# Attention and a Silu feed-forward on one core: all sums on VectorE, a redrawn order, and seven products for the first matmul of the last three batches

## The chip, the cores and the metric

One core of a Trainium2 chip. The time is that of one execution on the device, in microseconds (us), as the median of several runs. The profile is a hardware trace of one execution, whose span runs from the first to the last instruction of the program.

## The reference

Attention over 8 batches and 12 heads, 448 tokens of 64 values each, and then a feed-forward layer over the 3584 tokens with 768 values each:

```python
scores = q @ k.T / sqrt(64)              # per batch and head, 448 x 448
attn   = exp(scores - max) / sum(exp)
x      = attn @ v                        # heads side by side: 3584 x 768
h      = x @ w_in                        # 768 -> 2048
out    = (h * sigmoid(h)) @ w_out        # 2048 -> 768
```

Inputs and outputs are float32; the kernel loads them as float16 and sums in float32 in PSUM.

## The kernel before

**The work.** A unit is one batch with four of the twelve heads. Its k and q are loaded (L316, L322) and turned in 32x32 blocks on VectorE (L363, L374). Scores (L384) are matmuls with 32 rows of the array, four side by side; ScalarE takes Exp of two heads at once into a tile E (L409, 128x896). `attend` (L433) multiplies E by ones (part 0, the row sums) and by V (parts 1 and 2). To save part 0 one matmul in four, the first two chunks of E are added beforehand (`plan_esum`, two sums of 128x896 for a unit). VectorE inverts the sums (L455 to L460) and scales the result into xT (L466). Before this change the E sums could go to VectorE or GpSimd, whichever the plan found free.

**First feed-forward matmul.** `Plain` computes 128 rows of h for one batch as six matmuls of 128x128 by 448 (L486), then Tanh on ScalarE (L499) and a gate on VectorE, (tanh + 1) * x into G or, for some last 128 tokens of a pair of batches, X (L502). There are 16 such pieces in a batch. `Fold` is another way, which the code holds but does not use while `PLAIN = 8`: a 2x2 block form with seven products instead of eight, each of three matmuls of 224 columns, and eight folds in a batch. It needs four sums on the batch's x (`plan_t`), four on every slice of w_in (`plan_w_in_sums`, the tiles SI), and for each fold a copy, four additions with an operand in PSUM (y, c22, c12, c21) on VectorE, and a subtraction z on GpSimd (`ZENG`). The sums of w_in were made before this change too, although nothing read them.

**Second feed-forward matmul.** `Quad` does two tiles of 128 tokens by the same seven-product form: 56 matmuls of 384 columns (L805), four sums on G (tiles S, in two halves of 128x512, `plan_sums`), sums of w_out once (tiles TO, 16 sums of 128x768), and additions t and p on VectorE. In `VPS = (3, 4)` the third and fourth sums on G may go to GpSimd. Results go out through tiles t (L511, L515, L517) and stores (L546). All sums are issued by the helper `tt`, so they share line L511 and are told apart by their tiles.

**The order.** Every engine runs its instructions in the order in which the program emits them. That order comes from a plan at the end of the kernel: a class `Order` keeps a clock of its own, estimated durations (`mm`, `act`, `vec`, `half`, `pool`) and a time at which each engine is free, and starts the ready operation with the earliest time plus bias. It also keeps which buffers and PSUM banks are free. An operation of kind ANY goes to ScalarE or VectorE, one of kind VP to VectorE or GpSimd. Loads are issued on GpSimd, behind its sums. At the end all operations are emitted in the order of their planned start. The estimates set the order alone; on the chip, semaphores decide when each operation runs.

**Silu and the tables.** With `b >= SILU` a fold ends with ScalarE's Silu instead of Tanh and a gate. Silu isn't in the table of Exp and Tanh, so the plan issues no scores while more than `QB = 4` of a batch's Silu operations are left (`silu_phase`).

Of the kernel before, what the change touches and what calls it, by code (L numbers as in the profile page):

```python
# [18 lines left out]
DMA_RATE = 0.37  # L19
DMA_TAIL = 1.0  # L20
# [3 lines left out]


# [54 lines left out]
class Op:  # L80


    def __init__(self, eng, busy, emit, deps=(), bias=0.0, tail=HOP, then=None, table=None):
        self.eng, self.busy, self.emit = eng, busy, emit
        self.deps, self.bias, self.tail, self.then = list(deps), bias, tail, then
        self.table = table
        self.done = None
# [5 lines left out]
class Order:  # L93


    def __init__(self):
        self.now = 0.0
        self.free = {"PE": 1.2, "ACT": 2.1, "DVE": 1.2, "POOL": 1.2}
        self.wait = {"ACT": [], "DVE": [], "ANY": [], "POOL": [], "VP": []}
        self.pool = []  # L100
        self.dma_free = 0.0
        self.out = []
        self.mode = None
        self.table, self.loose = 0, True
        self.busy = {e: 0.0 for e in self.free}

    def add(self, op):
        self.wait[op.eng].append(op)
        return op

# [3 lines left out]
    def start(self, op, eng=None):  # L114
        eng = eng or op.eng
        busy = op.busy[eng] if isinstance(op.busy, dict) else op.busy
        if isinstance(op.busy, dict):
            self.emit(lambda: op.emit(eng))
        else:
            self.emit(op.emit)  # L120
        if op.table is not None:
            if op.table != self.table:
                self.table = op.table
                busy += TABLE
        self.free[eng] = self.now + busy
        self.busy[eng] += busy
        op.done = self.now + busy + op.tail
        if op.then:
            op.then(op.done)
# [7 lines left out]
    def load(self, mb, emit, ring=None):  # L137
        op = Op("POOL", 0.58, emit)
        self.pool.append((op, mb, ring))
        return op  # L140

    def step(self):

        soon = []
        for eng in ("ACT", "DVE"):
            if self.free[eng] > self.now:
                soon.append(self.free[eng])
                continue
            best, other = None, None
            for kind in (eng, "ANY") if eng == "ACT" else (eng, "ANY", "VP"):  # L150
                for op in self.wait[kind]:
                    at = op.ready()
                    if at is None:
                        continue
                    if at > self.now:
                        soon.append(at)
                    elif eng == "ACT" and op.table not in (None, self.table):
                        if (other is None or at < other[0]) and (self.table == 0 or self.loose):
                            other = (at, op)
                    elif best is None or at + op.bias < best[0]:  # L160
                        best = (at + op.bias, op)
            if other:
                best = other if not best or self.table == 0 and other[0] < self.now - PATIENCE else best
                if best is not other:
                    soon.append(other[0] + PATIENCE + 0.01)
            if best:
                self.wait[best[1].eng].remove(best[1])
                self.start(best[1], eng)
                soon.append(self.free[eng])
        work = None  # L170
        for kind in ("POOL", "VP"):
# [12 lines left out]
        elif self.pool:  # L184
            op, mb, ring = self.pool[0]
            at = 0.0
            if ring is not None:
                at = ring()
            if at is not None and at <= self.now:
                self.pool.pop(0)  # L190
                self.start(op)
                self.dma_free = max(self.dma_free, self.now + 1.5) + mb / DMA_RATE
                op.done = self.dma_free + DMA_TAIL
# [7 lines left out]
def kernel(  # L201
# [10 lines left out]

# [20 lines left out]
    DEFER, DITEM = .3, .1  # L233
    SUMS, EKEEP, ESENG = (0, 1), 2, 'VP'
# [4 lines left out]
    PLAIN = 8  # L239
    SILU = 8  # L240
# [3 lines left out]
    W_OUT_AT = NG * len(PIECES) + 6  # L244
    W_OUT_GAP = 2
# [21 lines left out]
    SI = {m: const.tile([128, HC, DFF // 2], FP16, name=f"SI{m}") for m in (1, 2, 4)}  # L267
# [5 lines left out]
    T_s = const.tile([128, 3, HC, S // 2], FP16, name="T")  # L273
    f_s = [const.tile([128, 3, S // 2], FP32, name=f"f_{i}") for i in range(NF)]
# [7 lines left out]
    def bank(i):  # L282
        return P_s[i // 2][:, 0] if i < 4 else B_s[i - 4]
# [16 lines left out]
    def rows_of(n, c):  # L300
        return KROWS[c] if form(*units[n][:2]) == "lone" else 128

# [114 lines left out]
    def attend(n, part, a, es, sums):  # L417
# [6 lines left out]
        for c in chunks:  # L424
            rest = c == NCH - 1 and what != "lone"
# [159 lines left out]
    def plan_k(b, hg):  # L585
        ld_k[(b, hg)] = od.load(1.2 * MB * TPP, lambda: load_k(b, hg), ringed("rk"))

    def plan_q(n):
        ld_q[n] = od.load(1.2 * MB * (units[n][3] - units[n][2]), lambda: load_q(n), ringed("rq"))
# [101 lines left out]
    VPS = (3, 4)  # L691
    WENG = 'VP'
# [14 lines left out]
    def bulk(out, u, w, how, deps, bias):  # L707
# [7 lines left out]
        return od.add(Op(WENG, busy, lambda eng: tt(out, u, w, how, eng), deps, bias))  # L715
# [34 lines left out]
    plan_w_in_sums()  # L750
# [3 lines left out]
    class Quad:  # L754
# [59 lines left out]
        def run(self):  # L814
# [5 lines left out]
            if m == 5:  # L820
# [3 lines left out]
                "PE", (i1 - i0) * mm(n), lambda: self.emit(m, a, m in (1, 5, 6), i0, i1), tail=PE_OUT  # L824
# [13 lines left out]
            def add(name, out, x, y, deps, then=None):  # L838
                ev[name] = od.add(
                    Op("DVE", vec(n), lambda: tt(out, x, y, ALU.add), deps, SLOW, then=then)  # L840
                )

            if m == 1:
                ev["p1"] = od.add(
                    Op("ANY", {"ACT": act(n), "DVE": vec(n)}, lambda e: copy(e, p, W), [op], SLOW)
# [5 lines left out]
            elif m == 6:  # L851
                add("y", W, Q, r, [op, ev["c11"]])
            elif m == 7:
# [9 lines left out]
    class Fold:  # L863
# [66 lines left out]
        def run(self):  # L930
# [14 lines left out]
            op = Op("PE", HC * mm(n), lambda: self.emit(m, a, c0, m in (1, 7)), tail=PE_OUT)  # L945
# [3 lines left out]
            def add(name, eng, out, u, w, how, deps, then=None):  # L949
                busy = vec(n) if eng == "DVE" else 0.12 + 0.00215 * n  # L950
                ev[name] = od.add(
                    Op(eng, busy, lambda: tt(out, u, w, how, eng), deps, SLOW, then=then)
# [3 lines left out]
            if m == 5:  # L956
# [4 lines left out]
                        lambda e: copy(e, F[:, 0:2], src), [op], SLOW,  # L961
                    )
                )
            elif m == 6:
                add("y", "DVE", y, A[:, n : 2 * n], p1, ALU.add, [op])
# [3 lines left out]
            elif m == 3:  # L969
                c12 = add("c12", "DVE", A[:, n : 2 * n], A[:, n : 2 * n], p1, ALU.add, [op])  # L970
                self.finish(A[:, 0 : 2 * n], self.f, [c12], True)
            elif m == 4:
                Bq = bank(self.banks[1])[:, 0:n]
                k = self.banks[1]
                c21 = add("c21", "DVE", p5, Bq, p5, ALU.add, [op, ev["z"]], lambda at: banks.give(k, at))
                self.finish(F[:, 1:3].rearrange("p i n -> p (i n)"), self.f + HF, [c21], False)
            if m in (6, 7) and self.at >= 5 and "c22" not in ev:
                Bq = bank(self.banks[1])[:, 0:n]
                add("c22", "DVE", y, Bq, y, ALU.add, [self.last7, ev["y"]] + [ev["z"]])

        def finish(self, src, ff, deps, psum):
# [9 lines left out]
            if b < SILU:  # L991
# [4 lines left out]
                        -0.3, tail=0.2, table=0,  # L996
# [3 lines left out]
                for lo, hi, dst, at in g_parts(b, 0, S):  # L1000
# [7 lines left out]
                            [last, clear], -4,  # L1008
# [5 lines left out]
            for lo, hi, dst, at in g_parts(b, 0, S):  # L1014
# [6 lines left out]
                        deps + [clear], -2, tail=0.2, table=1,  # L1021
# [14 lines left out]
    def plan_t(b):  # L1036
# [12 lines left out]
        def sums(out, u, w, deps):  # L1049
            return od.add(  # L1050
                Op("DVE", half(HC * n), lambda: tt(out, u, w, ALU.subtract), deps, SLOW + 2)
# [40 lines left out]
    def plan_sums(qd):  # L1092
# [7 lines left out]
        while sums_at[qd] < 4:  # L1100
# [16 lines left out]
            for f0 in (0, 4):  # L1117
# [9 lines left out]
                else:  # L1127
# [7 lines left out]
                        deps, SUM,  # L1135
# [7 lines left out]
    def tile_quad(qd):  # L1143
# [34 lines left out]
        def write(r, c, src, place, deps, then):  # L1178
            if r == 0:
# [5 lines left out]
                        deps, -4,  # L1185
# [21 lines left out]
    class Plain:  # L1207
# [20 lines left out]
        def run(self):  # L1228
# [4 lines left out]
            op = Op("PE", 2 * mm(t1 - t0), lambda: ffn1_plain(b, f, t0, t1, a, c0, c0 + 2), tail=PE_OUT)  # L1233
# [7 lines left out]
            done = od.add(Op("ACT", act(t1 - t0), lambda: tanh(x, th), [op], -0.3, tail=0.2, table=0))  # L1241
# [5 lines left out]
            for lo, hi, dst, at in g_parts(b, t0, t1):  # L1247
# [5 lines left out]
                    [done], -4,  # L1253
# [38 lines left out]
    def qk_at():  # L1292
# [6 lines left out]
        s = [max(banks.free[2 * y], banks.free[2 * y + 1]) for y in ys]  # L1299
# [5 lines left out]
    def run_qk():  # L1305
# [17 lines left out]
        )  # L1323
        done = []
# [8 lines left out]
        for y in ys:  # L1333

            def then(at, y=y):
# [11 lines left out]
                    table=0,  # L1347
                )
# [3 lines left out]
        if c in SUMS and c == SUMS[-1] and per_burst(n) == 1 and ys[-1] == 1:  # L1352
            plan_esum(n)
# [3 lines left out]
    def plan_esum(n):  # L1357
# [3 lines left out]
        at = sum_at[n] = e_slots.take(od.now)  # L1361
        made = sum_op[n] = []
        kr = rows_of(n, SUMS[-1])
        nq = 32 * (units[n][3] - units[n][2])
        for y in range(2):
            hs = slice(2 * y, 2 * y + 2)
            for i, c in enumerate(SUMS[1:]):
                u = e_at[n][SUMS[0]] if i == 0 else at
# [5 lines left out]
                            lambda eng, u=u, w=e_at[n][c], hs=hs: tt(  # L1374
                                E_s[at][0:kr, hs, 0:nq], E_s[u][0:kr, hs, 0:nq],
                                E_s[w][0:kr, hs, 0:nq], ALU.add, eng,
                            ),
                            deps, -2,
# [6 lines left out]
    def lent():  # L1385
        if not qk_seq or silu_phase() or LEND and e_slots.when(1) is None:
            return 0, 2
# [9 lines left out]

    def m_when(n):
        more = lent()
        at = sorted(banks.free[i] for i in (*M, *more))[n - 1]  # L1400
        return None if at == NEVER else at

    def m_take():
        more = lent()
        i = min((*M, *more), key=lambda i: (banks.free[i] > od.now, i < 4, banks.free[i]))
        assert banks.free[i] <= od.now
# [3 lines left out]
    def av_data():  # L1410
# [7 lines left out]
        if part == 0 and n in sum_op:  # L1418
            first = len(SUMS) - 1
# [18 lines left out]
    def run_av():  # L1438
# [5 lines left out]
        sums = SUMS if n in sum_op else ()  # L1444
        count = NCH - (len(sums) - 1 if sums and part == 0 else 0)
        op = Op("PE", count * mm(nq) + 0.013, lambda: attend(n, part, a, es, sums), tail=PE_OUT)
# [18 lines left out]
    def after_av(n, part, op, nq, a):  # L1465
        b, hg, g0, g1 = units[n]
        if part == 0:
# [3 lines left out]
            for step, busy in enumerate((nq / 960.0 + 0.13, 0.2, nq / 960.0 + 0.13)):  # L1471
# [5 lines left out]
                    -10,  # L1477
                )
# [4 lines left out]
        else:  # L1483
# [5 lines left out]
            def then(at):  # L1489
# [10 lines left out]
                then=then,  # L1500
            )
# [35 lines left out]
    def moe_pick(hold):  # L1537
# [3 lines left out]
        for item in moe[:60]:  # L1541
# [10 lines left out]
            at = max([at] + room)  # L1552
            need = 0
# [12 lines left out]
        return None, soon  # L1566

# [70 lines left out]
    for _, _, fn in sorted(od.out, key=lambda x: x[:2]):  # L1638
        fn()
# [30 lines left out]
```

The softmax here doesn't subtract the row's maximum and nothing guards it: scores larger than these inputs give would overflow.

## Time and profile before

| | |
|---|---|
| median of 3 runs | 447.63 us (444.66 to 449.26) |
| span of the profiled execution | 440.4 us |
| mean granted TensorE clock | 0.979 |
| sums on GpSimd, 128x896 / 128x512 / 128x384 (mean ns) | 1922 / 1157 to 1265 / 902 to 988 |
| the same shapes on VectorE, least ns | 604 / 355 / 344 |
| matmuls 128x448 of the plain pieces | 672, in 132.9 us |

"Busy" is time in which an engine executes. A busy TensorE is not one at its peak, since its matmuls are pipelined and their ends are modelled; spacing from start to start is the better measure of one. In the lists of groups, the time after the second bar is idle time of the engine ahead of those instructions, and the name after the arrow is whoever ended it. The engines are named PE (TensorE), DVE (VectorE), ACT (ScalarE), POOL (GpSimd) and SP (SyncE).

### The profile page before, as it was taken

The page shows a single profiled execution, that of the slowest core. Times are in us where ns is not written, and L with a number is a line of the kernel's source. Part 1 is how long each engine was busy: PE and PEld are TensorE (multiplying, and loading weights), DVE is VectorE, ACT ScalarE, POOL GpSimd, SP SyncE. Part 2 cuts the span into 40 slices and gives each one's busy share as a digit, 9 for nine tenths or more (in the row PEclk, how much of TensorE's full clock was granted, in tenths as well). Part 3 has the DMA queues.
Part 4 walks back from the last instruction along what each step waited for, and adds up shares of the span by engine and source line. Part 5 has one row for each costly group of instructions (what it writes and reads, how often), then busy time and mean ns, then how long its engine had stood idle before and what let it go on. Part 6 is the DMA issues. An engine that isn't in the chain of part 4 may idle for free.

```text
span 440.4 us, 9748 instructions
## 1 busy us (share of the span) xinstructions
PE 410.0 (93%) x3853; PEld 208.8 (47%) x3853; DVE 288.6 (66%) x565; ACT 233.8 (53%) x356; POOL 209.3 (48%) x277
## 2 busy tenths in 40 slices
PE   8998878999939999999999999999999999899985
PEld 7665544334315434544554434544453555455453
DVE  3536798777899776577557974587559635834751
ACT  3885757788800768466544755456856124214310
POOL 6575898977686354087204951065306100502510
PEclk9998989899988999999999999999999999999999
DMA  7999408599914456056510853118300130022023
GB/s 111 118 152 204 67 6 106 75 183 151 201 28 69 115 89 117 1 75 106 106 49 12 122 93 84 28 18 128 75 1 2 49 92 5 19 66 61 0 50 95
DMA packets 38750, 34.46 MB, mean 78 GB/s; under 512 B 11952, under 2 KB 37936, under 8 KB 38704
## 3 DMA queue, kind: packets, MB, share of 16 engines
q0 software_dynamic: 27952, 22.82, 37.0%
q1 hardware_dynamic: 9984, 10.24, 8.6%
q10 hardware_dynamic: 768, 0.79, 0.7%
q8 instruction: 30, 0.49, 0.4%
q14 instruction: 16, 0.13, 0.1%
HBM read 45.61 MB, written 11.01 MB: 129 GB/s over the span
## 4 chain that ended last, share of the span: by engine, by line
PE 60%; DVE 5%; DMA 2%; SPq 1%; issue 1%; POOL 1%; ACT 0%; DVEq 0%
PE p L486 24%; PE p L805 24%; PE p L433 7%; PE s L384 4%; DVE S L511 2%; DMA rk<-in_k_dram 1%; DVE E L511 1%; SPq L546 1%; DMA out_dram<-t 1%; DVE t L511 0%; POOL V L330 0%; DVE p L511 0%; DVE QT L374 0%; DVE G L502 0%; ACT th L499 0%
## 5 line engine op out<-in xcount | busy, mean ns | idle before, releaser
L409 ACT ACTIVATE E<-s 128x896 f16<-128x896 f32 (+1 forms) x172 | 148.6, 916 | 68.3 <-PE s L384 67.3
L486 PE MATMUL p<-xT,w_in_t 128*128 128x448 f16 (+1 forms) x864 | 156.9, 335 | 4.2 <-DVE G L502 3.2
L486 PEld LDWEIGHTS <-w_in_t 128*128 128x128 f16 x864 | 82.1, 99 | 76.9 <-issue 19.1
L502 DVE SCALAR_TENSOR_TENSOR G<-th,p 128x448 f16<-128x448 f16 (+2 forms) x144 | 75.7, 534 | 54.6 <-ACT th L499 54.1
L499 ACT ACTIVATE th<-p 128x448 f16<-128x448 f32 (+1 forms) x144 | 70.4, 507 | 63.7 <-PE p L486 60.5
L805 PE MATMUL p<-w_out_t,G 128*128 128x384 f16 x304 | 58.0, 327 | 1.9 <-DVE p L511 1.9
L384 PE MATMUL s<-QT,KT 32*128 32x448 f16 (+4 forms) x864 | 56.7, 343 | 3.0 <-ACT E L409 2.6
L511 POOL TENSOR_TENSOR G<-G 128x512 f16<-128x512 f16 x21 | 25.6, 1227 | 64.9 <-DVE S L511 64.3
L805 PEld LDWEIGHTS <-G 128*128 128x128 f16 x416 | 38.6, 98 | 36.1 <-issue 12.0
L330 POOL DMA_DIRECT2D V<-in_v_dram x88 | 48.9, 562 | 13.7 <-PE p L433 8.4
L515 ACT COPY t<-p 128x384 f32<-128x384 f32 x39 | 18.6, 479 | 69.3 <-PE p L805 67.0
L805 PE MATMUL p<-TO,S 128*128 128x384 f16 x192 | 39.3, 340 | 11.1 <-DVE S L511 7.6
L433 PE MATMUL p<-E,V 128*32 128x448 f16 (+2 forms) x848 | 43.9, 344 | 1.4 <-DVE xT L466 1.4
L805 PEld LDWEIGHTS <-S 128*128 128x128 f16 x280 | 25.8, 100 | 37.7 <-issue 15.5
L511 POOL TENSOR_TENSOR E<-E,E 128x896 f16<-128x896 f16 x18 | 34.6, 1922 | 18.0 <-ACT E L409 17.6
L511 DVE TENSOR_TENSOR t<-p,t 128x384 f32<-128x384 f32 x42 | 23.0, 549 | 29.3 <-PE p L805 26.6
L466 DVE SCALAR_TENSOR_TENSOR xT<-p,t 128x448 f16<-128x448 f32 (+1 forms) x53 | 29.8, 565 | 13.4 <-PE p L433 12.3
L384 PEld LDWEIGHTS <-KT 32*128 32x128 f16 (+2 forms) x864 | 17.6, 98 | 30.7 <-issue 29.0
L433 PEld LDWEIGHTS <-V 128*32 128x32 f16 (+1 forms) x864 | 20.3, 98 | 22.5 <-issue 12.4
L363 DVE STREAM_TRANSPOSE KT<-rk 128x256 f32<-128x256 f32 (+3 forms) x48 | 16.7, 385 | 19.6 <-DMA rk<-in_k_dram 19.6
L511 POOL TENSOR_TENSOR G<-X,G 128x512 f16<-128x512 f16 x4 | 4.9, 1216 | 46.2 <-DVE S L511 46.2
L455 DVE STREAM_TRANSPOSE t<-p 128x448 f32<-128x448 f32 (+1 forms) x27 | 15.9, 589 | 14.2 <-PE p L433 14.0
(62 smaller groups left out, 358.2 us busy)
## 6 DMA issues: line engine op xcount, KB each, us to landing
out_dram<-t SPq DMA_DIRECT2D x208, 48.0 KB, 1.6
rk<-in_k_dram POOLq DMA_DIRECT2D x24, 224.0 KB, 4.7
rq<-in_q_dram POOLq DMA_DIRECT2D x21, 224.0 KB, 5.4
w_out_t<-in_moe_w_out_dram POOLq DMA_DIRECT2D x8, 384.0 KB, 8.9
V<-in_v_dram POOLq DMA_DIRECT2D x43, 64.0 KB, 3.3
V<-in_v_dram POOLq DMA_DIRECT2D x40, 48.0 KB, 2.7
w_in_t<-in_moe_w_in_dram POOLq DMA_DIRECT2D x16, 96.0 KB, 4.7
w_in_t<-in_moe_w_in_dram POOLq DMA_DIRECT2D x8, 192.0 KB, 8.0
```

The source lines that it names most:

```text
L330: nc.gpsimd.dma_start(out=V[32 * x : 32 * (x + 1), hs, 0:count, :], in_=v[b, hs].rearrange("h (i g) d -> i h g d", g=TPP)[:, :, first : fi ...
L363: nc.vector.transpose(out=kt.rearrange("p c x i -> p x c i")[:, x:y, 0:count], in_=t[:, first : first + count * (y - x)].rearrange("p (x c ...
L384: nc.tensor.matmul(out=P_s[s_pair][p0 : p0 + 32 * (x1 - x0), h % 2, at : at + nq], lhsT=KT[(b, hg)][32 * h : 32 * (h + 1), c, x0:x1, :, e] ...
L409: nc.scalar.activation(out=E_s[e_i][0:kr, 2 * y : 2 * y + 2, 0:nk], in_=P_s[s_pair][0:kr, :, 0:nk], func=AF.Exp, scale=attn_scale,)
L433: nc.tensor.matmul(out=bank(a)[32 * h : 32 * (h + 1), 0:nq], lhsT=w, rhs=E_s[sum_at[n] if part == 0 and c in sums else es[c // per_burst(n)]][
L466: nc.vector.scalar_tensor_tensor(out=x_s[xi][:, cc % HC, 32 * g0 : 32 * g1], in0=bank(a)[:, 0:nq], scalar=0.5, in1=t_s[ti][:, 0:nq], op0=A ...
L486: nc.tensor.matmul(out=bank(a)[:, 0 : t1 - t0], lhsT=w_in_t[:, cc, 128 * f : 128 * (f + 1)], rhs=x_s[x_at[(b, cc // HC)]][:, cc % HC, t0:t ...
L499: nc.scalar.activation(out=th, in_=src, func=AF.Tanh)
L502: (nc.vector if eng == "DVE" else nc.gpsimd).scalar_tensor_tensor(out=out, in0=th, scalar=1.0, in1=x, op0=ALU.add, op1=ALU.mult)
L511: e.tensor_tensor(out=out, in0=a, in1=b, op=op)
L515: nc.scalar.copy(out=out, in_=in_)
L805: nc.tensor.matmul(out=bank(a)[:, 0 : self.n], lhsT=lhs(i), rhs=rhs(i), start=(start and i == 0), stop=(i == last), skip_group_check=True,)
```

## The change

It has four parts.

1. **All fp16 sums go to VectorE**: E sums, sums on G, of w_in and of w_out. GpSimd keeps loads, memsets and the small fp32 subtraction z of a fold. The aim is that the two engines don't hold each other up.
2. **The first feed-forward matmul of batches 5, 6 and 7 goes by seven products** (`PLAIN = 5`), to shorten TensorE's work, and ends in Silu (`SILU = 5`), so that VectorE has no gates there.
3. **The plan knows more**: at most 8 loads are open at a time and each lands at other estimated times; while VectorE and GpSimd would use their shared access the plan starts neither on top of the other; a PSUM tile in use by one engine isn't given to another. The order of all instructions follows from it.
4. **Small settings**: w_out is loaded one unit earlier and its halves in succession, `DEFER` is 0.15 instead of 0.3, and the second half of each score tile in PSUM can be lent to feed-forward work.

```diff
-DMA_RATE = 0.37
-DMA_TAIL = 1.0
+DMA_RATE = 0.4
+DMA_LAG = 2.4
+DMA_OPEN = 8
...
+    def locked(self, tiles, eng):
+
+        return max((t for i in tiles for e, t in self.lock[i].items() if e != eng), default=0.0)
...
+                    elif self.locked(op.tiles, eng) > self.now:
+                        soon.append(self.locked(op.tiles, eng))
+                    elif eng == "DVE" and op.port and self.port["POOL"] > self.now:
+                        soon.append(self.port["POOL"])
...
-        for kind in ("POOL", "VP"):
+        held = self.port["DVE"] > self.now or YIELD and any(
...
+        for kind in ("POOL", "VP") if not held else ():
...
-            if ring is not None:
+            if len(self.sent) >= DMA_OPEN and self.sent[-DMA_OPEN] > self.now:
+                at = self.sent[-DMA_OPEN]
+            elif ring is not None:
                 at = ring()
...
-                self.dma_free = max(self.dma_free, self.now + 1.5) + mb / DMA_RATE
-                op.done = self.dma_free + DMA_TAIL
+                self.dma_free = max(self.dma_free, self.now + DMA_LAG) + mb / DMA_RATE
+                op.done = self.dma_free
+                self.sent.append(op.done)
...
-    DEFER, DITEM = .3, .1
-    SUMS, EKEEP, ESENG = (0, 1), 2, 'VP'
+    DEFER, DITEM = .15, .1
+    EKEEP, ESENG = 2, 'DVE'
+    ES2 = 99
+    ES0, ES1 = 6, 99
...
-    PLAIN = 8
-    SILU = 8
+    PLAIN = 5
+    SILU = 5
...
-    W_OUT_AT = NG * len(PIECES) + 6
-    W_OUT_GAP = 2
+    W_OUT_AT = NG * len(PIECES) + 5
+    W_OUT_GAP = 1
...
     def bank(i):
-        return P_s[i // 2][:, 0] if i < 4 else B_s[i - 4]
+        return P_s[i // 2][:, i % 2] if i < 4 else B_s[i - 4]
...
+    def sums_of(n):
+        if per_burst(n) == 2 or n < ES0:
+            return ()
+        return (0, 1) if n < ES1 else (0, 1, 2) if n < ES2 else (0, 1, 2, 3)
...
-        od.load(1.2 * MB * TPP, lambda: load_k(b, hg), ringed("rk"))
+        od.load(MB * TPP, lambda: load_k(b, hg), ringed("rk"))
...
-    VPS = (3, 4)
-    WENG = 'VP'
+    VPS = ()
+    WENG = 'DVE'
...
-        return od.add(Op(WENG, busy, lambda eng: tt(out, u, w, how, eng), deps, bias))
+        return od.add(Op(WENG, busy, lambda eng: tt(out, u, w, how, eng), deps, bias, port=True))
...
     def lent():
         if not qk_seq or silu_phase() or LEND and e_slots.when(1) is None:
-            return 0, 2
+            return 0, 1, 2, 3
         return ()
```

The rest of the diff hands the PSUM bank of each operation to the plan (`bank=`), and marks sums as using the shared access (`port=True`).

## Prediction

> **What bounds the kernel now.** I read the page first, for who is busy:
>
> ```profile
> PE 410.0 (93%) x3853; PEld 208.8 (47%) x3853; DVE 288.6 (66%) x565; ACT 233.8 (53%) x356; POOL 209.3 (48%) x277
> PE   8998878999939999999999999999999999899985
> PE 60%; DVE 5%; DMA 2%; SPq 1%; issue 1%; POOL 1%; ACT 0%; DVEq 0%
> ```
>
> TensorE is the bound: 93% busy, and 60% of the chain that ended last. So a gain must shorten matmul work or one of TensorE's waits. The slices show one hole after the start, a 3 in the twelfth slice (121 to 132 us). The list of waits says whom TensorE waited for:
>
> ```profile
> PE p L805 <- DVE S L511: 7.6, 2, 7.0
> PE p L805 <- DVE t L511: 3.5, 2, 1.9
> PE p L486 <- DVE G L502: 3.2, 1, 3.2
> PE p L805 <- DVE p L511: 1.9, 3, 0.8
> PE p L433 <- POOL E L511: 1.7, 1, 1.7
> ```
>
> The columns are total, times, longest. One wait of 7.0 us stands out, and most of the others are waits for VectorE. The timeline of 104 to 150 us shows what made it; first VectorE, then GpSimd, then TensorE:
>
> ```profile
> 121.78 8.40 DVE L511 TENSOR_TENSOR w_out_t<-w_out_t 128x768 f16<-128x768 f16 x1
> 130.58 0.41 DVE L511 TENSOR_TENSOR S<-G 128x512 f16<-128x512 f16 x1
> ...
> 123.13 1.87 POOL L511 TENSOR_TENSOR E<-E,E 128x896 f16<-128x896 f16 x1
> 124.96 1.62 POOL L511 TENSOR_TENSOR TO<-w_out_t,TO 128x768 f16<-128x768 f16 x1
> 126.55 1.62 POOL L511 TENSOR_TENSOR w_out_t<-w_out_t 128x768 f16<-128x768 f16 x1
> 128.14 1.62 POOL L511 TENSOR_TENSOR TO<-w_out_t,TO 128x768 f16<-128x768 f16 x1
> ...
> 131.04 4.69 PE L805 MATMUL p<-TO,S 128*128 128x384 f16 x16 [6.97 <-DVE S L511]
> ```
>
> A single VectorE sum took 8.40 us, from 121.8 until GpSimd's chain of sums ended near 130. The same shape takes 0.55 us elsewhere (the TO<-w_out_t,TO group, mean 548 ns). TensorE's next operand is the S sum queued behind it. Groups kept apart by shape show that this is general:
>
> ```profile
> L511 POOL TENSOR_TENSOR E<-E,E 128x896 f16<-128x896 f16 x18 | 34.6, 1922 | 18.0 <-ACT E L409 17.6
> L511 DVE TENSOR_TENSOR E<-E,E 128x896 f16<-128x896 f16 x18 | 21.8, 1213 | 1.6 <-ACT E L409 1.6
> L511 DVE TENSOR_TENSOR S<-S,G 128x512 f16<-128x512 f16 x20 | 16.4, 835 | 0.2
> L511 DVE TENSOR_TENSOR t<-p,t 128x384 f32<-128x384 f32 x42 | 23.0, 549 | 29.3 <-PE p L805 26.6
> ```
>
> Sums with both inputs in SBUF have means far above their least times (E 604 ns, S<-S,G 355 to 416 ns by the lines' own answers), while t<-p,t, with one input in PSUM, keeps 496 to 559 ns. After the long wait TensorE also ran slow:
>
> ```profile
> 131.00:137.00 6.00, 5.96 (x25) 3.12 (x26) 5.80 (x11) 0.00 (x0) 5.09 (x6) 0.67 0.10 13
> ```
>
> The granted clock was 0.67 in these 6 us, so 6 x 0.33 = 2.0 us more.
>
> **What the Trainium skill says.** "SBUF — State Buffer", section "Who interferes with whom": a VectorE instruction with two SBUF inputs contends with a GpSimd instruction that reads SBUF, and the loser blocks rather than sharing. The trace agrees (8.40 us beside a GpSimd chain; 0.55 otherwise), and so does the unharmed PSUM sum. "TensorE: Matmul & The Clock Gate", section "The HAM clock gate": an idle window of about 3.4 us halves the clock; the 0.67 above fits. Its section "Wait — 56ns, not 53.3ns?" gives N/2.4 GHz plus about 2.5 ns for a warm matmul. The trace: 90 plain 448-wide matmuls from 397.8 to 414.9 us, 17.02 us by the chain of waits, 189 ns each, as stated (187 + 2.5). "ScalarE: Activation LUTs", section "What ACT_TABLE_LOAD costs", gives about 1283 ns; the only load here took 1283.
>
> **Part by part. (1) Sums leave GpSimd.** GpSimd ran 18 E sums, 38 sums of 128x512, 6 of 128x768 and 20 of 128x384, 109 us by its rows. On an undisturbed VectorE they cost 18 x 0.62 + 38 x 0.41 + 6 x 0.55 + 20 x 0.35 = 37 us. In exchange VectorE's own sums shrink to those prices: E 10.6, S<-S,G 8.5, w_out_t 8.8, S<-G 3.5, SI 4.3, the other rows with X and E about 6, together 41 us. So VectorE takes over all of it and comes out some 4 us lower. This hardly matters as a total; it matters on the path: the 7.0 us wait and its cold 2.0 us should go, **9 us**. The 16 w_out sums then need 16 x 0.55 = 9 us of VectorE before the first quads, but can spread behind the load, since matmuls of other kinds are there to run. Of the waits for VectorE or GpSimd that lie beside such overlaps (3.2 at 62.7 us, where SI sums took 1.0 us instead of 0.35; 1.9 at 384.5 us; 1.6 at 422 us; 1.7 for an E sum, in all 8.4) I count half, **4 us**.
>
> **(2) Seven products for the last three batches.** Plain: 96 matmuls of 448, 96 x 0.189 = 18.2 us a batch. Folded: 8 x 7 x 3 = 168 matmuls of 224. One costs 0.0957 us by the same rate; the timeline has twenty in 2.02 us (56.35 to 58.37 us), 0.101 with the switch at the end. So 16.1 to 17.0 us a batch, I take 16.1: three batches save **6.1 us** (3.6 at the other bound). SI sums were made before as well, unused, so they aren't new.
>
> Against it, VectorE in the three batches: 48 gates go (19.9 + 7.8 + 4.5 = 32.2 us in the groups of 300 to 441 us). There come 24 x 4 half-width additions from PSUM, at 0.388 us (the xT 128x224 row): 37.2; 12 sums on x of 128x672, 0.50 us between the 512 and 768 rows: 6.0; half of 24 copies at about 0.62: 7.4. Net +18 us in a stretch where VectorE was 80.35 us busy of 140.4. Per fold: TensorE 2.02 us, VectorE 1.55 + 0.25 + 0.31 = 2.1 us of duration, but queued VectorE instructions start some 0.08 us before the last one's listed end (130.11 + 0.55, next at 130.58), so about 1.7. ScalarE: two Silu near tanh's 0.547 and half a copy, 1.4. TensorE stays the bound, with little to spare and in a dependent chain: copy, y, z on GpSimd, c22, c21. Three open folds give 6 us of matmuls against a chain of some 4.6 us (seven products of 0.29 less those that run beside, and four or five steps of 0.4 to 0.6). I charge **1.3 us** a batch for filling and draining. A GpSimd z of 224 (about 0.5 us, scaled from the 0.91 of 128x384) may still hold up an S sum by that much; S sums wait little then.
>
> **(3) Silu.** Its table replaces that of Exp: two loads a batch, none back after the last, 5 x 1.283 = 6.4 us of ScalarE, which was 52.6 us busy of the last 140.4. TensorE feels it only where banks run out; I charge 0.3 us each, **1.5 us**. Silu itself isn't in the trace; between 0.5 and 0.6 us it changes nothing on the path. While a fold batch has over 4 activations left no scores are issued, so attention for batches 6 and 7 lies between fold batches, beside the quads (9 us of TensorE each, 56 x 0.163). Before, it ended near 340 us and the matmuls of batch 7 began at 397.8, so there are some 58 us of slack for two holds of 17 us.
>
> **(4) Order, loads, banks.** At most eight open loads, w_out one unit earlier, and the second PSUM half lent at the end: these move loads by a few us. TensorE waited 0.3 us for a load in all (the list of waits), so I cost them at nothing, hidden behind plain matmuls. The w_out halves back to back, 3.1 MB, may delay k and q once; that is in the range.
>
> Sum: -9 - 4 - 6.1 + 3.9 + 1.5 = -13.7. From the median of 447.6 this gives 434.
>
> **The rivals.** (a) All of it pays: all 8.4 us of waits go and folds fill well: 447.6 - 9 - 8.4 - 6.1 + 1 = 425. For: the overlap explains each of these waits. Against: a wait that is removed mostly uncovers the next. (b) The folds become VectorE-bound: at the full 2.1 us and transposes of attention between, 2.5 us a fold is 20 us a batch, 2 more than plain: -9 - 4 + 3 x 2 + 1.5 = 442. For: 2.1 against 2.02. Against: VectorE's pipelining. (c) Slower: folds run at 2.7 us, 21.6 a batch (+10 in all), the hold on scores leaves TensorE short by 3 us at each of two holds (+6), and half of the 9 us comes back at the first quads because all 16 w_out sums now queue on VectorE: 447.6 - 4.5 - 4 + 10 + 6 + 1.5 = 457. For: VectorE is in order and every chain now ends on it. Against: 66% busy, and little growth.
>
> **How the numbers follow.** The forecast 0.45 (429 to 438), (a) 0.20, (b) 0.19, (c) 0.16. The range holds the forecast, (a) down to 421 and (b), and the lower end of (c): 421 to 449. Faster by over 1% is below 443: the forecast, (a) and over half of (b), 0.76; within 1% (443 to 452) the rest of (b) and some of (c), 0.10; slower 0.14.
>
> **What would show it.** Right: no VectorE fp16 sum over about 1 us; no wait of TensorE over 3 us after 100 us; E and S sums at 0.62 and 0.41; GpSimd busy near 115 us, VectorE near 300; about 17 to 18 us from the first fold matmul of a batch to its last where nothing is woven in; five table loads after the first. Wrong: TensorE waits for c12, c21 or y of the folds over 4 us a batch, scores bunching behind Silu with waits on Exp, or a new wait at the first quads.

## The result and the profile after

The changed kernel took 419.65 us (median of 3 runs, 412.62 to 419.72) against 447.63: faster, ratio 0.928 with a 95% interval of 0.911 to 0.946. Measured again beside other kernels it took 414.69 us, ratio 0.936 (0.926 to 0.946). The ratios leave out executions that ran slow at a lower clock, so they differ a little from the ratio of the medians. The forecast was 434, with 421 as the low end: the direction was right, the gain of 28 us was twice what I had summed up.

The page after, in the order in which I read the page before: busy times, slices, clock, chain.

```profile
PE 396.2 (96%) x4052; PEld 226.8 (55%) x4052; DVE 293.9 (72%) x711; ACT 242.7 (59%) x381; POOL 116.8 (28%) x219
PE   8899899999999999999999999999999999999994
PE 77%; DMA 10%; DVE 6%; POOL 3%; issue 2%; ACT 0%; ACTq 0%; SPq 0%; DVEq 0%; POOLq 0%
```

The hole in the slices is gone, TensorE makes up 77% of the chain instead of 60%, and GpSimd has lost 92 us of work while VectorE has gained 5. VectorE near 300 and GpSimd near 115 us were forecast. The list of waits after, its four largest, with the same columns as before (total, times, longest):

```profile
PE p L836 <- DVE p L541: 1.9, 1, 1.9
PE p L1558 <- DVE zeros L289: 1.5, 1, 1.5
PE p L463 <- DMA V<-in_v_dram: 1.1, 1, 1.1
PE p L516 <- DVE t L485: 1.1, 3, 0.6
```

No wait of TensorE is longer than 1.9 us in this trace. The groups apart by shape show the sums at their undisturbed price, where the E sums on VectorE had 1213 ns and S<-S,G 835:

```profile
L541 DVE TENSOR_TENSOR E<-E,E 128x896 f16<-128x896 f16 x36 | 21.5, 616 | 0.3 <-ACT E L439 0.3
L541 DVE TENSOR_TENSOR S<-S,G 128x512 f16<-128x512 f16 x22 | 9.2, 418 | 0.1
```

Where the time came from is plainest in a table by stage. Two stretches of 44 us, first of the kernel before, then after; the columns are busy time and number of instructions of PE, PEld, DVE, ACT and POOL, then the granted clock, DMA share and GB/s.

```profile
44.00:88.00 44.00, 37.70 (x423) 20.05 (x421) 35.30 (x76) 30.85 (x55) 40.61 (x53) 0.92 0.48 64
88.00:132.00 44.00, 36.59 (x375) 14.81 (x374) 36.27 (x68) 28.12 (x40) 32.99 (x41) 0.96 0.94 141
```

```profile
44.00:88.00 44.00, 43.51 (x536) 23.61 (x538) 39.67 (x107) 34.81 (x60) 24.97 (x46) 1.00 1.01 149
88.00:132.00 44.00, 43.01 (x358) 19.84 (x351) 38.26 (x99) 23.10 (x34) 8.18 (x16) 1.00 0.53 91
```

In 88 us TensorE is busy for 86.5 instead of 74.3, and its clock no longer drops. So 12 us of idle time and some 5 us of slow clock (44 x 0.08 + 44 x 0.04) come from here alone, long before the first fold at 273.8 us.

### The profile page after: what moved, and what is told of

It is laid out like the page before. It is cut to its first block, busy times and chain, and to the rows that moved or that the text cites. A ratio compares the mean times of both kernels' runs of the same rounds, so it can differ in the third digit from the quotient of the medians.

```text
span 410.8 us, 10242 instructions
## 1 busy us (share of the span) xinstructions
PE 396.2 (96%) x4052; PEld 226.8 (55%) x4052; DVE 293.9 (72%) x711; ACT 242.7 (59%) x381; POOL 116.8 (28%) x219
## 4 chain that ended last, share of the span: by engine, by line
PE 77%; DMA 10%; DVE 6%; POOL 3%; issue 2%; ACT 0%; ACTq 0%; SPq 0%; DVEq 0%; POOLq 0%
PE p L836 28%; PE p L516 19%; PE p L463 9%; PE p L955 9%; PE s L414 8%; DMA rq<-in_q_dram 6%; DMA rk<-in_k_dram 3%; PE s L955 3%; POOL V L360 1%; DMA w_in_t<-in_moe_w_in_dram 1%; PE s L836 1%; POOL w_in_t L370 1%; DVE t L485 1%; PE s L463 1%; DVE TO L541 1%
## 5 line engine op out<-in xcount | busy, mean ns | idle before, releaser
L516 PE MATMUL p<-xT,w_in_t 128*128 128x448 f16 (+1 forms) x576 | 99.5, 322 | 4.1 <-DVE t L485 1.1
L529 ACT ACTIVATE th<-p 128x448 f16<-128x448 f32 (+1 forms) x96 | 44.8, 487 | 33.7 <-PE p L516 33.0
L532 DVE SCALAR_TENSOR_TENSOR G<-th,p 128x448 f16<-128x448 f16 (+2 forms) x96 | 48.0, 510 | 21.3 <-ACT th L529 21.0
L836 PEld LDWEIGHTS <-G 128*128 128x128 f16 x416 | 37.9, 98 | 36.3 <-issue 14.6
L836 PEld LDWEIGHTS <-S 128*128 128x128 f16 x312 | 28.6, 98 | 26.7 <-issue 9.2
L463 PE MATMUL p<-E,V 128*32 128x448 f16 (+3 forms) x800 | 40.3, 337 | 1.5 <-DMA V<-in_v_dram 1.1
L545 ACT COPY t<-p 128x384 f32<-128x384 f32 x27 | 12.9, 480 | 42.8 <-PE p L836 38.2
L836 PE MATMUL p<-TO,S 128*128 128x384 f16 x192 | 36.6, 327 | 0.0
L359 POOL MEMSET V<- 64x256 f16 x20 | 6.1, 305 | 92.6 <-PE p L463 92.2
L955 PE MATMUL p<-xT,w_in_t 128*128 128x224 f16 x165 | 23.2, 259 | 0.0
L541 DVE TENSOR_TENSOR E<-E,E 128x896 f16<-128x896 f16 x36 | 21.5, 616 | 0.3 <-ACT E L439 0.3
```

The lines of the kernel that those rows point to most:

```text
L463: nc.tensor.matmul(out=bank(a)[32 * h : 32 * (h + 1), 0:nq], lhsT=w, rhs=E_s[sum_at[n] if part == 0 and c in sums else es[c // per_burst(n)]][
L516: nc.tensor.matmul(out=bank(a)[:, 0 : t1 - t0], lhsT=w_in_t[:, cc, 128 * f : 128 * (f + 1)], rhs=x_s[x_at[(b, cc // HC)]][:, cc % HC, t0:t ...
L529: nc.scalar.activation(out=th, in_=src, func=AF.Tanh)
L532: (nc.vector if eng == "DVE" else nc.gpsimd).scalar_tensor_tensor(out=out, in0=th, scalar=1.0, in1=x, op0=ALU.add, op1=ALU.mult)
L541: e.tensor_tensor(out=out, in0=a, in1=b, op=op)
L836: nc.tensor.matmul(out=bank(a)[:, 0 : self.n], lhsT=lhs(i), rhs=rhs(i), start=(start and i == 0), stop=(i == last), skip_group_check=True,)
```

## The experiments

The times below are medians; "before" on the same chips was 444.9 to 446.5 us.

### The engine alone, and the setting

In the first kernel the order of before stays untouched and only the engine of the sums changes, in the helper `tt`:

```diff
-        e = nc.vector if eng == "DVE" else nc.gpsimd
+        e = nc.vector
```

> The kernel before with its planned order untouched; only where a sum was planned for GpSimd, VectorE issues it at the same place of the order. Nothing else changes (seven products stay unused). Theory C (contention: VectorE sums blocked by GpSimd cause the 7.0 us wait, the other waits for VectorE and, through them, most of the half-clock windows): no fp16 sum over 0.7 us, the 7.0 us wait and the clock windows after 60 us gone, about 20 us less, ratio 0.955. Rival P (the redrawn plan did most of it): only the one long wait goes, 9 us, ratio 0.98. Rival D (VectorE gets 37 us of work in an order drawn for two engines and TensorE waits for it elsewhere): ratio 1.0 or above.

Measured: 421.47 us, ratio 0.944 (0.940 to 0.948), 25 us less. Theory C holds, and more than in full; P and D fall. The E sums are at 614 ns and S<-S,G at 413. Span 419.5 us, clock 0.994. VectorE, which got all the sums, is busy for 275.6 us instead of 288.6. From 44 to 132 us TensorE is busy for 83.8 of the 88 us and its clock is 1.00, so most of what the two stretches above show comes with the engine alone. TensorE's three largest waits that are left:

```profile
PE p L433 <- DVE G L502: 2.4, 2, 2.0
PE s L384 <- ACT E L409: 2.1, 4, 1.0
PE p L1510 <- DVE zeros L264: 1.5, 1, 1.5
```

One rival had to be looked at here. The sums also stood ahead of the loads in GpSimd's queue, so the loads might have come too late before. The traces speak against it: VectorE sat idle until k and q arrived for 22.4 us before (19.6 and 2.8) and for 22.2 us in this kernel (18.8 and 3.4), and TensorE waited 0.3 us for loads in both.

In the second kernel the plan draws a new order for the same engines, still with its old knowledge:

```diff
-    SUMS, EKEEP, ESENG = (0, 1), 2, 'VP'
+    SUMS, EKEEP, ESENG = (0, 1), 2, 'DVE'
-    VPS = (3, 4)
-    WENG = 'VP'
+    VPS = ()
+    WENG = 'DVE'
```

> The kernel before with the three settings that send sums to VectorE alone, so the old plan, which knows nothing of shared access, open loads or PSUM tiles, draws its order for it. Theory C: ratio 0.955 as with the order untouched, within 0.01 of it. Rival P: 0.98, and a further 0.02 needs the new plan. Rival D: 1.0 or above.

Measured: 425.86 us, ratio 0.954 (0.950 to 0.958). This is 4.4 us more than with the order that was drawn for two engines. Redrawing by the old plan isn't what pays.

### Work that nobody reads

```diff
-    plan_w_in_sums()
+    if PLAIN < B:
+        plan_w_in_sums()
```

> The kernel before without the w_in sums that nothing reads (20 on GpSimd, 12 on VectorE). Theory C: the 3.2 us wait at 62.7 us and the half-clock window beside it go, about 5 us, ratio 0.988; the 7.0 us wait at the w_out sums stays. Rival P: ratio 1.0.

Measured: 446.13 us, ratio 1.002 (0.999 to 1.006). My expectation failed: taking 20 sums off GpSimd and 12 off VectorE brought nothing. In its trace the order has shifted, and other sums meet: two w_out sums took 1.73 and 3.67 us from 111.8 us on, and TensorE waited 3.1 us for a gate (X) behind them. With sums left on both engines, less work here only moved the places where they collide.

### Contention put back

The changed kernel with the sums free to go to either engine, as before; folds and new plan stay:

```diff
-    EKEEP, ESENG = 2, 'DVE'
+    EKEEP, ESENG = 2, 'VP'
-    VPS = ()
-    WENG = 'DVE'
+    VPS = (3, 4)
+    WENG = 'VP'
```

> The changed kernel with the three settings for sums set back, so E sums, w_out and w_in sums and two of the four sums on G may go to GpSimd again; the new plan still draws the order, starts GpSimd sums only where it believes VectorE isn't using the shared access, and the folds stay. Theory C: what the plan believes is off by tenths of a microsecond, VectorE sums are blocked again; 10 us or more above the changed kernel, ratio to before 0.96 or above. Rival P (the plan's knowledge keeps them apart): within 3 us of the changed kernel.

Measured: 438.35 us, ratio 0.983 (0.979 to 0.986), some 20 us above the changed kernel. The plan's own idea of the shared access doesn't keep the two apart on the chip. Its timeline, VectorE's and GpSimd's sums from one place:

```profile
125.46 1.17 POOL L541 TENSOR_TENSOR G<-G 128x512 f16<-128x512 f16 x1
125.52 4.70 DVE L541 TENSOR_TENSOR TO<-w_out_t,TO 128x768 f16<-128x768 f16 x1
126.58 3.22 POOL L541 TENSOR_TENSOR TO<-w_out_t,TO 128x768 f16<-128x768 f16 x2
```

Again a VectorE sum starts while GpSimd is at one and ends only when GpSimd's run of sums ends.

Next, contention and nothing else. The base is the changed kernel without folds (`PLAIN = SILU = 8`), which leaves room in SBUF for two small tiles:

> The changed kernel with PLAIN = SILU = 8: no seven products, no w_in sums; all else of the change stays. If the folds give their full 6.1 us once no sum is on GpSimd: 6 us more than the changed kernel, ratio to before 0.944. If folds fill badly (my charge of 5.4 us): no more than 1 us above it, 0.931. If the new plan is worth much by itself, this kernel is well under the 0.944 that the engine change alone reached.

Measured: 424.45 us, ratio 0.958 (0.949 to 0.968). The new plan without folds is no faster than the engine change alone. With folds, in the same set, the kernel took 414.69, 9.8 us less; by the ratios (0.936 and 0.958) 10 us, each with an interval of 4 to 5 us to each side. Part of this is clock. Three of the four executions without folds had a granted clock of 0.959 to 0.962 and took 423.65 to 425.56 us; the changed kernel at 0.958 and 0.959 took 419.65 to 421.81. Near 0.98 it is 421.06 against 415.91 and 417.65. Both comparisons leave about 4 us for the folds, an estimate: more than the 0.7 that my charges of 5.4 left of the 6.1, and less than all of it. On this base one kernel has a GpSimd sum, the other two GpSimd memsets ahead of each of the 16 w_out sums, on tiles of their own:

```diff
+    def disturb(bias):
+        if bias == TB:
...
+            nc.gpsimd.tensor_tensor(out=DD[i], in0=DD[i], in1=DD[i], op=ALU.subtract)
```

> The kernel without folds of this same set, and ahead of each of the 16 w_out sums on VectorE a GpSimd subtraction of 128x768 fp16 on a tile of its own that nothing else reads: only contention is added. Theory C: some of the w_out sums and their neighbours take 1.5 us and more, TensorE waits for VectorE by 3 to 8 us between 85 and 110 us, 5 to 10 us more than without, ratio to before 0.96. Rival (GpSimd's occupation delays loads, or nothing is on the path): the sums stay at 0.55 us, under 2 us more.

> The same, but GpSimd writes zeros twice to its own 128x768 tile instead of subtracting: it is about as long occupied, but reads nothing. If contention is for reads, as the skill says: the sums on VectorE stay at 0.55 us and the time within 1 us of the kernel without them. If GpSimd's occupation as such hurts (loads issued late behind it): as slow as with the subtractions.

Measured: 433.34 us with sums (ratio 0.975, 0.960 to 0.991) and 430.05 with memsets (0.968, 0.953 to 0.984): 8.9 and 5.6 us more than without. With sums, VectorE is blocked as theory C says. Its timeline, of GpSimd, VectorE and TensorE:

```profile
93.14 2.90 POOL L746 TENSOR_TENSOR D<-D 128x768 f16<-128x768 f16 x2
93.44 3.02 DVE L544 TENSOR_TENSOR TO<-w_out_t 128x768 f16<-128x768 f16 x1
96.51 0.48 PE L847 MATMUL p<-TO,S 128*128 128x384 f16 x2 [1.78 <-DVE TO L544]
```

A sum of 0.55 us took 3.02, through two GpSimd sums, and TensorE waited 1.78 us for it. With memsets every TO sum keeps 550 to 555 ns, so it is reading that blocks, as the Trainium skill, "SBUF — State Buffer" (section "Who interferes with whom"), has it. But the second half of my expectation failed: the memsets cost time in another way. Lines of GpSimd, VectorE and TensorE:

```profile
103.95 20.64 POOL L745 MEMSET D<- 128x768 f16 x28
128.22 0.70 DVE L394 STREAM_TRANSPOSE KT<-rk 128x192 f32<-128x192 f32 x2 [9.56 <-DMA rk<-in_k_dram]
129.48 2.08 PE L846 MATMUL p<-TO,S 128*128 128x384 f16 x6 [7.82 <-DVE xT L497]
```

A load of k was issued behind 20.64 us of memsets, at 124.5 us instead of 114.9; VectorE's turn of it came late, and what was queued behind that turn (xT) held TensorE for 7.8 us. So work on GpSimd has two costs: its reads block VectorE's sums, and its length delays the loads behind it. The 8.9 us can't be divided between the two: near the same clock the sums cost hardly more than the memsets (427.26 us at 0.992 and 426.35 at 0.988, 433.22 at 0.960 and 433.13 at 0.956). That blocking lengthens the kernel isn't shown by this pair, but by the 1.78 us here and the 7.0 us wait before.

### Folds and Silu

Folds alone, on the kernel before (`PLAIN = SILU = 5`, sums on either engine):

> The kernel before with seven products and Silu for batches 5 to 7, sums on either engine as before. If folds fill without waits whatever else is done: 6.1 us less, ratio 0.986. If GpSimd's sums hurt the folds too (z and the sums on G share GpSimd and block VectorE's sums on x): the gain is lost, ratio 1.0 to 1.02, with waits of TensorE for VectorE in the last 130 us.

Measured: 446.78 us, ratio 0.998 (0.995 to 1.002). The gain is eaten, though mainly not in the last 130 us, where I had expected it: from 44 to 132 us TensorE is busy for 68.9 us instead of 74.3. The redrawn order puts an E sum where the w_out sum had been:

```profile
120.40 10.45 DVE L511 TENSOR_TENSOR E<-E,E 128x896 f16<-128x896 f16 x1
```

10.45 us for 0.62, under five GpSimd sums and an E sum in a row, and a TensorE wait of 9.3 us. Both settings under the old plan, sums as in the second kernel and folds:

> The kernel before with both settings, all sums on VectorE and folds for batches 5 to 7, under the old plan. If the two parts explain the change: the 425.9 us of the sums alone less the folds' 6 us, 420 us, ratio 0.94, and the new plan is worth the rest of some 4 us. If folds need the new plan's knowledge of PSUM tiles to fill well: 426 us or more.

Measured: 424.18 us, ratio 0.957 (0.950 to 0.964), 1.7 us below the sums alone by the medians and no better by the ratios (0.957 and 0.954). So under the old plan folds bring little or nothing, even with no sum on GpSimd. What differs from the changed kernel is then the plan and the small settings. Taken apart from both sides:

```diff
-    DEFER, DITEM = .15, .1
-    W_OUT_AT = NG * len(PIECES) + 5
-    W_OUT_GAP = 1
-            return 0, 1, 2, 3
+    DEFER, DITEM = .3, .1
+    W_OUT_AT = NG * len(PIECES) + 6
+    W_OUT_GAP = 2
+            return 0, 2
```

> The changed kernel with the small settings as before: DEFER 0.3, w_out one unit later and its halves apart, only the first half of each score tile lent. If the new plan's knowledge makes the folds fill: within 3 us of the changed kernel. If the settings do: near the 424 us that sums and folds reach under the old plan.

> Sums on VectorE and folds under the old plan, which took 424 us, with the small settings of the change (DEFER 0.15, w_out earlier and its halves in succession, both halves of the score tiles lent). If the settings carry the difference: near 415. If the plan's knowledge does: 422 or more, the lent halves possibly making it worse[...].

Measured: the changed kernel with the old settings 424.27 us (0.950, 0.945 to 0.955); the old plan with the new settings 421.61 (0.945, 0.940 to 0.950). The first of the two gives a wrong output (relative error 0.051), presumably because in its order one operation comes ahead of another that it should follow, so its time proves nothing here. By the second, the settings under the old plan are worth 3 us by the medians and 5 by the ratios, with intervals that touch; what is left to the changed kernel, 7 us by the medians and 4 by the ratios, comes with the plan's knowledge. How the two share under the new plan stays open. One place can be named. In the kernel with sums and folds under the old plan TensorE waited 2.3 us for the w_out sums at the first quads (122 us) and lost clock (0.92 from 110 to 132 us); with the new settings, which load w_out earlier, it has no wait for a w_out sum.

Now why folds depend so much on their surroundings. Two variants of the changed kernel, first without Silu (`SILU = 8`, gates on VectorE), then with folds from batch 3 on:

> The changed kernel with SILU = 8 and gates on VectorE: the folds stay, but end in Tanh and a gate, without table loads and without holding back scores. VectorE gets 48 gates, about 29 us, in the last 130. If Silu's table loads and the hold cost what I charged (1.5 us): no gain from dropping them, since VectorE is then the tighter engine in the folds: 0 to 5 us more. If the hold matters: 2 us less.

> The changed kernel with seven products and Silu from batch 3 on. If folds give their full 2.05 us each batch: 4 us less than the changed kernel, ratio to before 0.925. If the hold on scores now starves TensorE, since batches 3 and 4 fold while most of the attention of later batches is still to be done: 0 to 8 us more.

Measured: 440.15 us (0.985, 0.975 to 0.995) and 443.32 us (0.989, 0.985 to 0.993), 25 and 29 us above the changed kernel by the medians, far beyond both expectations. Part of the second is clock: at 0.983 it took 435.73 and 436.10, some 19 us above the changed kernel near 0.98. The second one's timeline shows its first fold batch, TensorE only:

```profile
210.45 0.45 PE L955 MATMUL p<-xT,w_in_t 128*128 128x224 f16 x3 [1.08 <-ACT f L545]
...
212.95 0.45 PE L955 MATMUL p<-T,w_in_t 128*128 128x224 f16 x3 [0.78 <-DVE f L541]
...
215.11 0.45 PE L955 MATMUL p<-xT,w_in_t 128*128 128x224 f16 x3 [1.14 <-ACT f L545]
```

A fold every 4.66 us (210.45 to 215.11) for 2.0 us of matmuls: only one is open, and TensorE waits for each link of its chain, the copy (ACT f) and the additions (DVE f). The tile is f throughout. A second fold would have to borrow an E tile, and scores had taken them all. If that is so, leaving E tiles free must cure it:

```diff
-        e = e_slots.when(1) if ys[0] == 0 else 0.0
+        e = e_slots.when(4 if any(isinstance(x, Fold) for x in moe[:20]) else 1) if ys[0] == 0 else 0.0
```

> The changed kernel with seven products from batch 3 on, as in the run that took 443 us, and one more rule: scores leave three E tiles free while a fold is among the next 20 items of feed-forward work, since a fold that finds its only own tile f taken borrows an E tile. If the first fold batch starved because scores held all E tiles (one fold at a time, 4.66 us each): the starving goes, some 20 us come back, 420 to 425 us. If something else made it slow (table loads, VectorE): it stays above 435.

Measured: 420.27 us, ratio 0.939 (0.932 to 0.946): 23 us came back by the medians, some 16 between executions at clocks of 0.983 and 0.984. The fold matmuls of its first fold batch now follow one another, TensorE only:

```profile
203.48 0.45 PE L955 MATMUL p<-xT,w_in_t 128*128 128x224 f16 x3
203.77 0.45 PE L955 MATMUL p<-T,SI 128*128 128x224 f16 x3
204.05 0.45 PE L955 MATMUL s<-T,w_in_t 128*128 128x224 f16 x3
```

The starving was for E tiles. It still doesn't beat the changed kernel: two more fold batches should save 4 us of matmuls, yet TensorE is busy for 397.7 us, against 396.2, and idle for 17.0, against 14.6. And Tanh with the hold of scores and the lent banks that Silu has:

> The changed kernel with folds that end in Tanh and a gate on VectorE, as in the run that took 440 us, but scores are held back and PSUM banks lent during fold batches just as with Silu. If Silu helped through the hold (E tiles and banks left to the folds): back to within 5 us of the changed kernel. If it helped by sparing VectorE the 48 gates: stays at 435 or above. Between the two, about 430, if both.

Measured: 433.59 us, ratio 0.971 (0.965 to 0.976), 6.6 us less than without the hold, with intervals that just overlap, and still 14 to 19 above the changed kernel. But the output of this kernel is wrong (relative error 0.279), again presumably by its order, so it is a hint and no proof. It points to both: the hold leaves E tiles and banks to the folds, and Silu spares VectorE the gates, perhaps the larger part. Shown is only what they do together: the kernel with Tanh and no hold, whose output is right, is 25 us slower. In the kernel with Tanh and the hold VectorE was busy 112.75 us of the last 152, in the changed one 100.59 of the last 147.

In the changed kernel itself the folds run without a gap. Its timeline in batch 5, and the same stretch by engine:

```profile
286.23 0.45 PE L955 MATMUL p<-xT,SI 128*128 128x224 f16 x3
286.51 0.45 PE L955 MATMUL p<-T,w_in_t 128*128 128x224 f16 x3
286.80 0.45 PE L955 MATMUL p<-T,SI 128*128 128x224 f16 x3
...
286.20:299.20 13.00, 13.00 (x137) 12.93 (x135) 10.27 (x29) 9.11 (x28) 3.96 (x6) 1.00 0.15 39
```

Three matmuls every 0.287 us, 0.0957 each, as forecast; VectorE is busy 10.3 of 13 us, so the folds have it near its limit but not at it.

## Why the prediction was wrong

**The mechanism was right.** GpSimd's sums blocked VectorE's, the 7.0 us wait and the cold clock behind it went, VectorE's load hardly grew, and the folds' matmuls cost 0.0957 us each. The order-untouched kernel has the first of these without folds and without a new order. What failed is the size of three terms.

**Mis-sized term one: part (1), "9 us" plus "4 us".** It measured 25 us with the order untouched and 21 with the order redrawn by the old plan. I counted the long wait, 2.0 us of slow clock after it and half of the other waits. By the profiles of before and of the order-untouched kernel the granted clock alone gives 440.4 x 0.021 = 9.2 us less 419.5 x 0.006 = 2.5, so 6.7 instead of 2.0: the slices of 44 to 88 us had lost clock too (0.92), and I had not priced those, though the page's clock line showed them. The long wait of 7.0 and all 8.4 us of the others, not half, make 22.1 with it, against a span that is 20.9 us shorter. My reason for halving, that "a wait that is removed mostly uncovers the next", didn't hold: some waits stayed or came (2.0 us for a gate), but TensorE's idle time fell by 15.2 us in all (30.4 to 15.2). It did hold where the source stayed, in the kernel without unused sums.

**Mis-sized term two: parts (2) and (3), charges of 3.9 and 1.5 us.** In the changed kernel TensorE waited 0.2 us in fold matmuls (its list of waits), so the charges were about nothing there; of the 6.1 us some 4 came near the same clock, and where the rest went stays open. My chain of 4.6 us was right (4.66 measured for a lone fold), and open folds do hide it. What I missed is that this hangs on E tiles, and on gates or the hold: the same folds cost some 20 to 25 us more with Tanh or two batches earlier. I named Silu's hold only as a risk (rival c); whether it is a help is hinted at, not shown. Of the smaller estimates, z took 0.66 us and not 0.5, and VectorE came out 13.0 us lower with the engine alone, not "some 4".

**Mis-sized term three: part (4), costed at nothing.** I wrote "these move loads by a few us" and hid them behind plain matmuls. The kernel with parts (1) to (3) under the old plan and settings took 424.18 us, so the rest of the change, what (4) covers, measured 9.5 us. Little of it lies in the folds, whose matmuls waited 1.4 us there and 0.2 in the changed kernel. By the two profiles, with clocks of 0.994 and 0.996, the first fold starts 6.1 us later there (279.9 and 273.8), out of a span that is 10.5 us longer, and TensorE is busy for 82.0 of the 88 us from 44 to 132, not 86.5. Which setting or which knowledge does it stays open beyond the w_out sums named above.

**The rivals.** Rival (a), 425, was nearest: the waits went and folds filled. It lacked the clock and part (4). The slow folds of rivals (b) and (c) appear in the Tanh and batch-3 variants, but in the second for want of E tiles, which neither rival names.

## What to carry to other kernels

Before giving elementwise work to GpSimd to relieve VectorE, look whether VectorE's instructions with two SBUF inputs get longer beside it; here an estimated 37 us of sums moved onto VectorE left it 13 us less busy and made the kernel 25 us shorter. When waits share one cause, count them and the slow clock behind them in full. When a step needs several open chains to fill TensorE, count the buffers that each chain takes and who else takes them, since a chain left alone runs at its own latency.

## What the runs showed of the hardware

- A blocked VectorE sum doesn't wait for one GpSimd instruction but for a run of them: 8.40 us, 10.45 us and, in a kernel built for it, 3.02 us through two sums that took 2.90 together.
- GpSimd memsets of nearly as long a total (22.7 us, the sums 26.1) left VectorE's sums at 0.55 us, but delayed a load by 9.6 us.
- The granted clock differs between executions of one kernel: four of the changed kernel had 0.959 to 0.996, with 412.5 to 421.8 us. A gain of under 2% needs several executions here.
- A busy TensorE isn't always granted the full clock. In the profiled execution of the kernel without folds the clock was 0.50 from 12 to 44 us, with TensorE busy for 31.8 of these 32 us; in the changed kernel's it was 0.95 in the same stretch, with TensorE busy for 28.3. What decides it no run here shows.
